# Polysketch attention and PReLU MLP on one core: the last MLP group written by token, and a fixed order of operations

## The chip, the core and the metric

The kernel runs on one core of a Trainium2 chip. A core has five engines, each with its own queue of instructions: TensorE (PE in the profile) multiplies matrices and writes to PSUM, eight banks of 128 x 512 fp32; VectorE (DVE), ScalarE (ACT) and GpSimd (POOL) work element by element; SyncE (SP) starts DMA transfers here, as ScalarE does for a few. An instruction waits in its queue until what it depends on is done, and everything behind it on that engine waits with it. The metric is the time of the program on the device in microseconds, median over runs.

## What is computed

Linear attention with a polynomial sketch for 4 batches of 4 heads, 1088 tokens, head dimension 32; then an MLP over all 4352 tokens (128 -> 2048 -> 128) with a PReLU whose slope alpha differs by hidden unit.

```python
def phi(x):
    a = np.einsum('rd,bhsd->bhsr', S1, x)
    b = np.einsum('rd,bhsd->bhsr', S2, x)
    return np.einsum('bhsi,bhsj->bhsij', a, b).reshape(*x.shape[:-1], r * r)
q_p, k_p = phi(q), phi(k)
num = np.einsum('bhsf,bhfd->bhsd', q_p, np.einsum('bhsf,bhsd->bhfd', k_p, v))
den = np.einsum('bhsf,bhf->bhs', q_p, np.sum(k_p, axis=2))[..., None] + 1e-06
x = (num / den).transpose(0, 2, 1, 3).reshape(B * S, H * D)
h = x @ w_in
out = (np.maximum(h, 0) + alpha * np.minimum(h, 0)) @ w_out
```

## The kernel before

**Algebra.** PReLU is alpha h + (1 - alpha) relu(h). So the kernel prepares W = w_in diag(alpha) w_out, a 128 x 128 matrix, and w_out scaled by 1 - alpha, and computes relu(x w_in) w_out' + x W.

**Attention, by batch.** `keys` transposes k in 32 x 32 blocks on VectorE, applies the sketches ("ab", on TensorE with small tiles of its array), forms phi on GpSimd, a Gram matrix for the sum of phi(k) ("gram"), and phi(k)^T v ("kv", L519), which is transposed ("tz") and copied to `kvw`. `queries` does the same for q ("qabc"), divides by the denominator, forms phi(q) and multiplies by kvw ("num", L610). The result is copied as bf16 into `xT`, 128 features by 4352 tokens (L619). Batch 0's queries are two units, the others one each.

**MLP, by group of tokens.** `GROUPS` are eight groups of 512 columns of xT and a last one of 256. For each of the 16 blocks of hidden units: a matmul of w_in's block with xT into one of the banks H0 to H2 (L633; A0 to A3 too in the last two groups), a relu into a bf16 buffer rh on ScalarE (L640) or VectorE (L642), and a matmul with w_out's block that accumulates in bank O (L646). A 17th matmul adds x W (L653). Bank O then holds the output with features on partitions; VectorE transposes it in 32 x 32 blocks into a buffer oT (L658), and four DMAs, one for each 32 features, write it in rows of 128 bytes (L670); a group that spans two batches needs eight. All are on SyncE's queue, but for two of the last group's, which are on ScalarE's.

**Preparation.** w_in is cast to bf16 in four pieces on ScalarE (L412). It is also transposed by TensorE in four pieces (L430), scaled by alpha into winT on VectorE or ScalarE (L438, L441), and multiplied by w_out (L448) into W, whose cast is on ScalarE (L451). w_out is scaled in L420 and L423.

**Order.** Every operation is an `Op` with engines, a duration, dependencies and the buffers that it takes. `schedule` picks one after the other: of those that could start first by its own clock, the one with the smallest number in `ORDER`; it also picks the engine and the buffer, and fills TensorE's gaps early in the program with matmuls on zeros (L382). The instructions are then issued in that order, so each engine's queue holds it. Loads of later batches are held back by tiny VectorE writes ("gates", L356) into their destination.

Of the kernel before, what the change touches and what calls it, by code (L numbers as in the profile page):

```python
# [12 lines left out]
BF16 = mybir.dt.bfloat16  # L13
# [15 lines left out]
SLACK = {"ACT": 140, "PE": 0, "DVE": 170}  # L29
# [3 lines left out]
ORDER = [  # L33
# [48 lines left out]
STICK = {"PE": 5000}  # L82


def schedule(ops, slots, filler=None):
# [4 lines left out]

    free_at = {"DVE": 830, "PE": 900, "POOL": 700, "ACT": 700}
    cfg, glued = "full", None
# [4 lines left out]
    def slot_free(s):  # L97
        h = holder[s]
        if h is None:
            return slot_at[s]  # L100
        if any(o.end is None for o in h.frees) or not h.frees:
            return None
        return max(o.end + 150 for o in h.frees)

    waits = {id(o): sum(d.end is None for d in o.deps) for o in ops}
    users = {}
    for o in ops:
        for d in o.deps:
            users.setdefault(id(d), []).append(o)
    ready = [o for o in ops if waits[id(o)] == 0]  # L110
    order = []
    while ready:
        best = None
        known = {}
        for o in ready:
            t0 = 0
            picks = []
            ok = True
            taken = set()
            for h in o.takes:  # L120
                for s in h.names:
                    if s not in known:
                        known[s] = slot_free(s)
                cand = sorted((known[s], s) for s in h.names if known[s] is not None and s not in taken)
                if len(cand) < h.n:
                    ok = False
                    break
                chosen = cand[:h.n]
                taken |= {s for _, s in chosen}
                picks.append([s for _, s in chosen])  # L130
                t0 = max([t0] + [t for t, _ in chosen])
            if not ok:
                continue
            for e, dur in o.eng.items():
                if e == "PE":
                    if glued is not None and o is not glued:
                        continue
                    if o.cfg != cfg:
                        dur += SWITCH
                    if free_at.get("PE", 0) < COLD and not o.warm:  # L140
                        dur *= 2
                t = max(t0, free_at.get(e, 0))
                if o.port and e in ("DVE", "POOL"):
                    t = max(t, free_at.get("PORT", 0))
                for d in o.deps:
                    t = max(t, d.end + (0 if d.on == e else d.lat if d.on == "DQ" else d.lat + SLACK.get(e, 0)))
                if e == "PE":
                    for i, (limit, at) in enumerate(have):
                        if issued + o.ni > limit:
                            t = max(t, have[i + 1][1])  # L150
                o_key = (t, o.prio, t + dur)
                if best is None:
                    best = []
                best.append((t, o.prio, t + dur, o, e, dur, picks))
        assert best, "no operation can start"

        t_first = min(b[0] for b in best)
        near = [b for b in best if b[0] <= t_first + 60]
        t, _, end, o, e, dur, picks = min(near, key=lambda b: (
            b[1] - (STICK["PE"] if b[4] == "PE" and b[3].cfg == cfg != "full" else 0), b[2]))  # L160
        if e == "PE" and filler and 4000 < free_at.get(e, 0) < FILL:
            each = 430 if free_at[e] < COLD else 215
            n = int((t - free_at[e] - 40) / each)
            idle = [s for s in FILL_BANKS if slot_free(s) is not None and slot_free(s) <= free_at[e]
                    and s not in sum(picks, [])]
            if n > 0 and idle:
                x = filler(n, idle[-1], each)
                x.behind = [f for f in holder[idle[-1]].frees] if holder[idle[-1]] else []
                x.end, x.on, x.took = free_at[e] + each * n, e, each * n
                order.append((free_at[e], e, x))  # L170
                slot_at[idle[-1]] = x.end
                holder[idle[-1]] = x.takes[0]
                issued += x.ni
                cfg = x.cfg
# [3 lines left out]
        if e == "PE":  # L178
            issued += o.ni
            cfg, glued = o.cfg, o.glue  # L180
            if issued > have[-1][0] - 256:
                have.append((have[-1][0] + 256, max(end, free_at.get("DQ", 0)) + 2600))
        for h, names in zip(o.takes, picks):
            h.got = names
            o.behind += [f for s in names if holder[s] for f in holder[s].frees]
            for s in names:
                holder[s] = h
        order.append((t, e, o))
        ready.remove(o)
        for u in users.get(id(o), ()):  # L190
            waits[id(u)] -= 1
            if waits[id(u)] == 0:
                ready.append(u)
# [5 lines left out]
def kernel(  # L199
# [12 lines left out]
    nc = tc.nc  # L212
# [511 lines left out]
```

## Time and profile before

| | |
|---|---|
| median of 3 runs | 106.33 us (105.56 to 108.42) |
| profiled execution | 106.62 us, span 103.9 us |
| busy: PE, weight loads, DVE, ACT, POOL | 96.5, 52.0, 71.3, 71.3, 43.3 us |
| granted TensorE clock | 0.998 |
| DMA | 11.24 MB, 22863 packets, 19008 of them under 512 bytes |
| the chain that ended last | PE 71%, DMA 8%, DVE 8%, SyncE's queue 6% of the span |

The span runs from the first instruction to the last; the profiled execution's time holds some 2.7 us more around it. Matmuls are pipelined: the record of one of 512 columns lasts 0.38 us, and the next starts 0.22 us after it, so PE's busy time covers short waits. Idle time of an engine that is not the bottleneck costs nothing.

### The profile page before, as it was taken

What the parts mean: (1) busy time and instruction counts of PE and PEld (TensorE: products, weight loads), DVE (VectorE), ACT (ScalarE), POOL (GpSimd) and SP (SyncE); (2) the same over time, 40 slices, a digit from 0 to 9 for tenths busy, and PEclk for the clock granted to TensorE, in tenths of its full rate; (3) what the DMA queues carried; (4) which work ended last, traced back from release to release, by engine and by line L of the source; (5) the groups of instructions that cost most, each with busy time, mean ns of one, the idle gap of its engine ahead of it and who ended that gap; (6) DMA issues with size and microseconds to landing.
All of it is one profiled execution on the core that took longest, in us unless ns stands there. A gap on an engine that the chain in (4) does not pass through costs nothing.

```text
span 103.9 us, 3351 instructions
## 1 busy us (share of the span) xinstructions
PE 96.5 (93%) x1364; PEld 52.0 (50%) x1375; DVE 71.3 (69%) x154; ACT 71.3 (69%) x157; POOL 43.3 (42%) x47
## 2 busy tenths in 40 slices
PE   5978999999999999999999997999999999999950
PEld 4637789544653444446453444444444344444740
DVE  3556999997999994867867963892365544654740
ACT  1331998396676996664967952899798898694820
POOL 4009619499937999099159629700000000000000
PEclk9999999999999999999999999999999999999999
DMA  2999974965200777075002380140033060032243
GB/s 64 311 218 362 415 288 137 290 199 172 102 0 6 109 227 197 11 125 192 0 0 40 60 212 17 26 75 0 6 47 54 0 95 9 7 61 36 39 65 51
DMA packets 22863, 11.24 MB, mean 108 GB/s; under 512 B 19008, under 2 KB 21056, under 8 KB 22848
## 3 DMA queue, kind: packets, MB, share of 16 engines
q1 hardware_dynamic: 21952, 10.95, 40.5%
q8 instruction: 10, 0.16, 0.6%
q10 hardware_dynamic: 896, 0.08, 0.6%
q14 instruction: 5, 0.04, 0.1%
HBM read 8.80 MB, written 2.23 MB: 106 GB/s over the span
## 4 chain that ended last, share of the span: by engine, by line
PE 71%; DMA 8%; DVE 8%; SPq 6%; issue 3%; ACT 1%; ACTq 0%
PE O L646 24%; PE H L633 23%; SPq L305 6%; PE A L610 5%; DMA q_sb<-in_q_dram 5%; PE A L633 3%; DMA v_sb<-in_v_dram 3%; PE H L519 3%; PE O L448 3%; PE A L555 2%; DVE winT L438 2%; PE O L653 2%; PE A L469 1%; PE A L519 1%; PE A L499 1%
## 5 line engine op out<-in xcount | busy, mean ns | idle before, releaser
L640 ACT ACTIVATE rh<-H 128x512 bf16<-128x512 f32 (+1 forms) x96 | 50.8, 595 | 8.1 <-PE H L633 6.5
L633 PE MATMUL H<-xT,w_in_bf 128*128 128x512 bf16 (+1 forms) x122 | 40.0, 374 | 0.4 <-DVE ab L476 0.2
L646 PE MATMUL O<-rh,w_out_bf 128*128 128x512 bf16 (+1 forms) x135 | 39.8, 366 | 0.4 <-issue 0.2
L642 DVE TENSOR_SCALAR rh<-H 128x512 bf16<-128x512 f32 (+1 forms) x28 | 18.3, 658 | 7.1 <-PE H L633 5.9
L633 PEld LDWEIGHTS <-w_in_bf 128*128 128x128 bf16 x144 | 13.7, 99 | 16.4 <-issue 3.2
L484 POOL TENSOR_TENSOR phi<-ab 128x576 f32<-128x576 f32 x15 | 17.3, 1179 | 10.7 <-DVE ab L476 10.7
L646 PEld LDWEIGHTS <-w_out_bf 128*128 128x128 bf16 x144 | 13.9, 98 | 15.2 <-issue 1.7
L590 POOL TENSOR_TENSOR qf<-qa 128x1152 f32<-128x1152 f32 (+2 forms) x9 | 17.0, 1908 | 3.6 <-DVE qa L583 3.3
L658 DVE STREAM_TRANSPOSE oT<-O 128x512 f32<-128x512 f32 (+1 forms) x9 | 6.1, 683 | 9.6 <-PE O L646 7.1
L596 DVE STREAM_TRANSPOSE qp<-qf 128x1152 f32<-128x1152 f32 (+2 forms) x10 | 11.1, 1119 | 0.0
L561 DVE STREAM_TRANSPOSE qa<-A 128x288 f32<-128x288 f32 (+2 forms) x20 | 7.0, 395 | 2.2 <-PE A L555 2.2
L640 ACT ACTIVATE rh<-A 128x512 bf16<-128x512 f32 (+1 forms) x13 | 5.8, 514 | 2.6 <-PE A L633 2.5
L382 PE MATMUL O<-warm 128*128 128x256 bf16 x36 | 6.3, 338 | 1.1 <-DVE warm L364 1.1
L610 PE MATMUL A<-qp,kvw 32*32 32x288 f32 (+2 forms) x320 | 7.1, 364 | 0.0
L461 DVE STREAM_TRANSPOSE kT<-k_sb 128x544 f32<-128x544 f32 x8 | 5.6, 720 | 1.6 <-DMA k_sb<-in_k_dram 1.5
L619 ACT CAST xT<-A 128x128 bf16<-128x128 f32 (+3 forms) x12 | 3.3, 332 | 4.9 <-PE A L610 4.9
L412 ACT CAST w_in_bf<-w_in_f 128x512 bf16<-128x512 f32 x4 | 4.4, 1147 | 3.2 <-DMA w_in_f<-in_moe_w_in_dram 3.2
L546 DVE STREAM_TRANSPOSE qT<-q_sb 128x544 f32<-128x544 f32 (+2 forms) x10 | 5.7, 602 | 1.0 <-DMA q_sb<-in_q_dram 1.0
L583 POOL TENSOR_TENSOR qa<-qa,rd 128x288 f32<-128x288 f32 (+1 forms) x4 | 2.5, 630 | 8.6 <-DVE rd L582 6.3
L619 DVE CAST xT<-A 128x288 bf16<-128x288 f32 (+2 forms) x8 | 2.9, 392 | 3.7 <-PE A L610 3.7
L610 PEld LDWEIGHTS A<-qp,kvw 32*32 32x32 f32 x320 | 3.9, 103 | 2.8 <-issue 1.3
L382 PEld LDWEIGHTS <-warm 128*128 128x128 bf16 x36 | 4.1, 121 | 2.2 <-DVE warm L364 1.1
(80 smaller groups left out, 86.7 us busy)
## 6 DMA issues: line engine op xcount, KB each, us to landing
k_sb<-in_k_dram SPq DMA_DIRECT2D x3, 544.0 KB, 4.7
q_sb<-in_q_dram SPq DMA_DIRECT2D x3, 544.0 KB, 4.1
out_dram<-oT SPq DMA_DIRECT2D x20, 64.0 KB, 2.0
v_sb<-in_v_dram SPq DMA_DIRECT2D x8, 144.0 KB, 3.7
v_sb<-in_v_dram SPq DMA_DIRECT2D x8, 128.0 KB, 4.0
w_in_f<-in_moe_w_in_dram SPq DMA_DIRECT2D x2, 512.0 KB, 6.7
w_out_f<-in_moe_w_out_dram SPq DMA_DIRECT2D x2, 512.0 KB, 5.5
k_sb<-in_k_dram SPq DMA_DIRECT2D x2, 272.0 KB, 3.0
```

The source lines that it names most:

```text
L305: getattr(nc, eng).dma_start(dst, src)
L382: nc.tensor.matmul(bank[name][:, :256], warm[:, :128], warm[:, :256], start=True, stop=True)
L484: eng.tensor_mul(bufs[hph.got[0]][:, rr_, :, h2].rearrange("p w (i j) -> p w i j", i=r), view(src, [[64, KW], [1, r], [0, r]], 32 * rr_ + ...
L561: ta.append(op(("DVE", dve(n)), lambda h=h: nc.vector.transpose(bufs[hqa.got[0]][:, h * n:(h + 1) * n], bank[hA[h].got[0]][:, :n]), prio + ...
L590: side(e).tensor_mul(bufs[hqf[rr_].got[0]][:, :4 * n].rearrange("p (m i j) -> p m i j", i=r, j=r), view(src, [[32, 2 * nb], [1, r], [0, r] ...
L596: mu.append(op(("DVE", dve(4 * n) + 40), lambda rr_=rr_: nc.vector.transpose(bufs[hqp[rr_].got[0]][:, :4 * n], bufs[hqf[rr_].got[0]][:, :4 ...
L610: nc.tensor.matmul(bank[hX[c].got[0]][32 * h:32 * (h + 1), :n], kvw[b][32 * c:32 * (c + 1), i, 32 * h:32 * (h + 1)], view(bufs[hqp[h // 2] ...
L619: x_done[x0] = (w, op({"ACT": act(w), "DVE": dve(w)}, lambda e, c=c, w=w, x0=x0: copy(e)(xT[:, x0:x0 + w], bank[hX[c].got[0]][:, :w]), lat ...
L633: hm = op(("PE", n / 2.4 + 3), lambda c=c, hh=hh: nc.tensor.matmul(bank[hh.got[0]][:, :n], w_in_bf[:, c * 128:(c + 1) * 128], xT[:, col0:c ...
L640: nc.scalar.activation(bufs[hr.got[0]][:, :n], bank[hh.got[0]][:, :n], ACTF.Relu)
L642: nc.vector.tensor_scalar_max(bufs[hr.got[0]][:, :n], bank[hh.got[0]][:, :n], 0.0)
L646: nc.tensor.matmul(bank["O"][:, :n], w_out_bf[:, c], bufs[hr.got[0]][:, :n], start=state["n"] == 0, stop=state["n"] == last)
```

## The change

**The last group's output is computed by token.** For the last 256 columns, the relu's result is the stationary operand and w_out's block the moving one: two matmuls of 128 columns for each of 16 blocks, and two for x W, each half into a bank of its own with 128 tokens on partitions. No transpose follows: each half is copied to a buffer and written by one DMA in rows of 512 bytes, the first from SyncE and the second from ScalarE. So that the tokens of a half lie well in the output, the last 256 columns of xT are permuted when they are copied from PSUM, which splits that copy in two. In the first eight blocks both halves are one operation, in the last eight two. The last group may use bank O for its hidden units, and there are twelve rh buffers instead of ten.

**The order is written out.** `ORDER` goes, and `PLAN` lists all 719 operations by number, with the engine where there is a choice (a, d, p). `schedule` walks through the list and assigns buffers by its own clock.

**Dependencies.** ScalarE's copies that may come first (`c_wq`, `c_g`, `c_win`) depend on `c_tab`, the copy that stands behind the table load, and the first entries of the plan are the loads of the sketch rows and of alpha.

```diff
-ORDER = [
-    -2000, -1990, 2, 3, 4, 5, 6, 7, 8, 9, 20000, 7003, 1007, 4992, -17950, 7045, 20000, 8112, -7780, -9037,
...
+PLAN = """
+    14 13 12 10 19 18 2 56 0 1 11 20 21 22 3 57 58 59 60 27 4 143 144 65 66 5 15 6 61p 63p 28 29 23 67 68d 32 41
...
+    order = []
+    for word in plan.split():
+        o = ops[int(word.rstrip("adp"))]
+        e = names[word[-1]] if word[-1] in names else next(iter(o.eng))
...
-    P_rh = pool("rh", 10, [128, 512], BF16)
+    P_rh = pool("rh", 12, [128, 512], BF16)
...
+            tail = GROUPS[-1][1] if x0 + w == T else 0
+            def f_x(e, c=c, w=w, x0=x0, tail=tail):
+                x = bank[hX[c].got[0]]
+                copy(e)(xT[:, x0:x0 + w - tail], x[:, :w - tail])
+                if tail:
+                    copy(e)(view(xT, [[128, tail // 128], [1, 4], [4, 32]], T - tail),
+                            x[:, w - tail:w].rearrange("p (t j i) -> p t j i", j=4, i=32))
...
+        hT = [Hold(ABANKS + ["O"]), Hold(ABANKS + ["O"])]
+        def by_token(i, x, w):
+            nc.tensor.matmul(bank[hT[i].got[0]][:, :DM], x, w, start=done[i] == 0, stop=done[i] == last)
+            done[i] += 1
...
+            def f_t(c=c, hr=hr, parts=(0, 1)):
+                for i in parts:
+                    by_token(i, bufs[hr.got[0]][:, 128 * i:128 * (i + 1)], w_out_bf[:, c])
...
+            for i, ts in enumerate((t0, t1)):
+                ho = Hold(P_ob)
+                ev = op({"DVE": dve(DM), "ACT": act(DM)}, lambda e, i=i, ho=ho: copy(e)(
+                    bufs[ho.got[0]][:, :4].rearrange("p a b -> p (a b)"), bank[hT[i].got[0]][:, :DM]),
+                    prio - 5, deps=os_ + ts, takes=[ho], frees=[hT[i]])
+                def f_rows(i=i, ho=ho):
+                    b, x = B - 1, col0 + 128 * i - (B - 1) * S
+                    dma(("sync", "scalar")[i], dram(out, (b * S + x // 32) * DM, [[NB * DM, 32], [1, 4 * DM]]),
+                        bufs[ho.got[0]][:, :4].rearrange("p a b -> p (a b)"))
```

**Where the order differs: ScalarE before the first relus.** Line numbers are those of each kernel. winT is w_in transposed and scaled, kvs and kvw are batch 0's copies, rh are relu buffers, A, H and O PSUM banks. Before:

```order
L412 CAST w_in_bf<-w_in_f 128x512 x3
L423 ACTIVATE w_out_bf<-w_out_f,oma 128x128 x4
L412 CAST w_in_bf<-w_in_f 128x512
L441 ACTIVATE winT<-H_104,al 128x128 x4
L423 ACTIVATE w_out_bf<-w_out_f,oma 128x128 x4
L451 CAST W_bf<-O 128x128
L619 CAST xT<-A_101 128x128
L619 CAST xT<-A_103 128x128
L619 CAST xT<-A_102 128x128
L640 ACTIVATE rh_130<-H_104 128x512
```

Now, from the second winT chunk on (a cast of w_in and one chunk stand ahead of it):

```order
L417 ACTIVATE winT<-O,al 128x128 x4
L417 ACTIVATE winT<-H_105,al 128x128 x4
L499 COPY kvs_116<-H_104 128x256
L388 CAST w_in_bf<-w_in_f 128x512
L508 COPY kvw_96<-H_106 128x256
L373 COPY Wq_90<-ST 128x16
L399 ACTIVATE w_out_bf<-w_out_f,oma 128x128 x4
L388 CAST w_in_bf<-w_in_f 128x512
L599 CAST xT<-A_102 128x128
L599 CAST xT<-A_100 128x128
L388 CAST w_in_bf<-w_in_f 128x512
L630 ACTIVATE rh_130<-H_106 128x512
```

Three winT chunks and the copies of batch 0 have come to ScalarE, one set of w_out's scalings and W's cast have moved behind the first relus, and three of the four w_in casts now stand behind the scalings.

**SyncE around batch 3's v (v_sb_73).** The oT writes here are those of the group that spans two batches, and after the change those of group 1. Before:

```order
L305 DMA q_sb<-in_q_dram 128x1088
L305 DMA out_dram<-oT_142 32x2x32 x4
L305 DMA out_dram<-oT_142 32x14x32 x4
L305 DMA v_sb_73<-in_v_dram 32x4x288
L305 DMA v_sb_73<-in_v_dram 32x4x256
L305 DMA v_sb_73<-in_v_dram 32x4x288
L305 DMA v_sb_73<-in_v_dram 32x4x256
```

Now:

```order
L281 DMA k_sb_69<-in_k_dram 128x1088
L281 DMA out_dram<-oT_143 32x16x32 x4
L281 DMA q_sb<-in_q_dram 128x1088
L281 DMA v_sb_73<-in_v_dram 32x4x288
L281 DMA v_sb_73<-in_v_dram 32x4x256
L281 DMA v_sb_73<-in_v_dram 32x4x288
L281 DMA v_sb_73<-in_v_dram 32x4x256
L281 DMA out_dram<-oT_144 32x2x32 x4
L281 DMA out_dram<-oT_144 32x14x32 x4
```

The loads of q and v of batch 3 stand behind one group's four writes, which precede them, and ahead of the writes of the group that spans two batches.

**SyncE and TensorE at the end.** oT_140 to oT_144 are output buffers. SyncE before:

```order
L305 DMA out_dram<-oT_142 32x16x32 x4
L305 DMA out_dram<-oT_140 32x6x32 x4
L305 DMA out_dram<-oT_140 32x10x32 x4
L305 DMA out_dram<-oT_141 32x16x32 x4
L305 DMA out_dram<-oT_142 32x8x32 x2
```

And now:

```order
L281 DMA out_dram<-oT_143 32x16x32 x4
L281 DMA out_dram<-oT_142 32x6x32 x4
L281 DMA out_dram<-oT_142 32x10x32 x4
L281 DMA out_dram<-oT_143 32x4x128
L281 DMA out_dram<-oT_144 32x16x32 x4
```

The first token half's write (4 x 128 in each of 32 rows) stands ahead of the four of group 7. TensorE's last rows before:

```order
L646 LDWEIGHTS w_out_bf
L646 MATMUL O<-rh_132,w_out_bf 128x256
L646 LDWEIGHTS w_out_bf
L646 MATMUL O<-rh_133,w_out_bf 128x256
L653 LDWEIGHTS W_bf
L653 MATMUL O<-xT,W_bf 128x256
```

And now, from group 7's last output matmul (L636) on; ten matmuls of the token halves (L617, into A_101 and A_102) follow it, of which the first five stand here:

```order
L636 LDWEIGHTS w_out_bf
L636 MATMUL O<-rh_130,w_out_bf 128x512
L617 LDWEIGHTS rh_135
L617 MATMUL A_102<-w_out_bf,rh_135 128x128
L617 LDWEIGHTS rh_136
L617 MATMUL A_101<-w_out_bf,rh_136 128x128
L617 LDWEIGHTS rh_133
L617 MATMUL A_101<-w_out_bf,rh_133 128x128
L617 LDWEIGHTS rh_139
L617 MATMUL A_101<-w_out_bf,rh_139 128x128
L617 LDWEIGHTS rh_141
L617 MATMUL A_101<-w_out_bf,rh_141 128x128
```

Group 7's accumulation ends close to the program's end. On VectorE its transpose is the last instruction, and ScalarE's last three are the two halves' copies and the second half's write.

More of the change, by code (lines that the diff above doesn't have):

```diff
@@ L102, in slot_free @@
             return None
[L103 to L107, printed above, removed]
-        for d in o.deps:
[L109 to L174, printed above, removed]
@@ new lines, in slot_free @@
+        return max(o.end + 100 for o in h.frees)
+    order = []
+    for word in plan.split():
+        o = ops[int(word.rstrip("adp"))]
+        e = names[word[-1]] if word[-1] in names else next(iter(o.eng))
+        dur = o.eng[e]
+        t, picks, taken = 0, [], set()
+        for h in o.takes:
+            cand = sorted((t_, s) for t_, s in ((slot_free(s), s) for s in h.names if s not in taken) if t_ is not None)
+            assert len(cand) >= h.n, "no buffer is free"
+            taken |= {s for _, s in cand[:h.n]}
+            picks.append([s for _, s in cand[:h.n]])
+            t = max([t] + [t_ for t_, _ in cand[:h.n]])
+        if e == "PE":
+            if o.cfg != cfg:
+                dur += SWITCH
+            if free_at["PE"] < COLD and not o.warm:
+                dur *= 2
+        t = max(t, free_at[e])
+        if o.port and e in ("DVE", "POOL"):
+            t = max(t, free_at["PORT"])
+        for d in o.deps:
+            t = max(t, d.end + (0 if d.on == e else d.lat))
+        if e == "PE":
+            for i, (limit, at) in enumerate(have):
+                if issued + o.ni > limit:
+                    t = max(t, have[i + 1][1])
+            if 4000 < free_at[e] < FILL:
+                each = 430 if free_at[e] < COLD else 215
+                n = int((t - free_at[e] - 40) / each)
+                idle = [s for s in FILL_BANKS if slot_free(s) is not None and slot_free(s) <= free_at[e]
+                        and s not in sum(picks, [])]
+                if n > 0 and idle:
+                    x = filler(n, idle[-1], each)
+                    x.behind = list(holder[idle[-1]].frees) if holder[idle[-1]] else []
+                    x.end, x.on, x.took = free_at[e] + each * n, e, each * n
+                    order.append((free_at[e], e, x))
+                    holder[idle[-1]], slot_at[idle[-1]] = x.takes[0], x.end
+                    issued += x.ni
+        end = t + dur
```

102 lines of the change are left out of this document (68 added, 34 removed), and 14 rows, old and new, of the table ORDER.

## The prediction

> **What bounds the kernel now.** I read the busy time by stages first, to see which engine a stage belongs to. The columns are the stretch's length and then the busy time (and instructions) of PE, of its weight loads, of DVE, ACT and POOL; the 1.00 is the granted clock.
>
> ```profile
> 10.00:20.40 10.40, 10.23 (x266) 8.36 (x266) 10.01 (x29) 8.54 (x20) 5.63 (x7) 1.00 0.81 288
> 20.40:60.00 39.60, 38.87 (x645) 18.93 (x645) 33.40 (x75) 29.63 (x65) 29.38 (x25) 1.00 0.39 97
> 60.00:66.00 6.00, 5.33 (x148) 2.99 (x148) 2.81 (x7) 2.72 (x8) 4.13 (x3) 1.00 0.35 96
> 66.00:96.00 30.00, 29.75 (x193) 13.31 (x194) 16.55 (x25) 25.10 (x50) 0.86 (x1) 1.00 0.23 36
> 96.00:100.20 4.20, 4.15 (x35) 3.11 (x32) 2.79 (x8) 3.00 (x10) 0.00 (x0) 1.00 0.41 64
> ```
>
> From 10 us, when the first half of w_in has landed, until the last matmul at 100 us, TensorE is the bound: it is idle 0.17 + 0.73 + 0.67 + 0.25 + 0.05 = 1.87 us of 90.2. The granted clock is 1.00 throughout. No reordering can therefore win more than about two microseconds there; the remaining places are the 3.9 us after the last matmul and the 10 us before w_in.
>
> The chain of waits (start, length, what) shows the largest of the idle pieces, at 62.7 us: batch 3's kv matmuls (L519) wait for its v, whose four loads stand in SyncE's queue behind eight output writes, which stand behind a transpose of VectorE.
>
> ```profile
> 53.12 0.73 DVE oT L658
> ...
> 59.96 3.27 DMA v_sb<-in_v_dram
> 63.37 1.40 PE H L519 x72
> ```
>
> The end, from the timeline: last matmul, transpose of the output, two writes on each of two queues. The row below it gives KB and microseconds from issue to landing.
>
> ```profile
> 99.87 0.27 PE L653 MATMUL O<-xT,W_bf 128*128 128x256 bf16 x1
> 100.18 0.45 DVE L658 STREAM_TRANSPOSE oT<-O 128x256 f32<-128x256 f32 x1 [0.66 <-PE O L653]
> 100.66 0.81 SPq L305 DMA_DIRECT2D out_dram<-oT  x2
> 100.67 0.88 ACTq L305 DMA_DIRECT2D out_dram<-oT  x2
> ...
> out_dram<-oT ACTq DMA_DIRECT2D x2, 32.0 KB, 1.8
> ```
>
> Count everything from P, the start of the last matmul (99.87). The last issue starts at about 100.67 + 0.88/2 = 101.1, that is P + 1.2, and lands 1.8 us on, at P + 3.0; the span's other 1.0 us is the program's end, the same in both kernels.
>
> **The change, part by part.** The profiled execution took 106.62 us for a span of 103.9; the median of the runs is 106.33. I sum in the profile's time and take 0.3 off for the median at the end.
>
> *The head, up to the first MLP matmul.* The new order moves the scaling of w_in's transposes (winT) from three on VectorE and one on ScalarE to one and three, and puts the last four W matmuls behind the attention's first outputs.
>
> ```profile
> 10.03 3.26 ACT L412 CAST w_in_bf<-w_in_f 128x512 bf16<-128x512 f32 x3 [3.23 <-DMA w_in_f<-in_moe_w_in_dram]
> 13.19 1.27 ACT L423 ACTIVATE w_out_bf<-w_out_f,oma 128x128 bf16<-128x128 f32 x4
> 15.42 1.12 ACT L441 ACTIVATE winT<-H,al 128x128 f32<-128x128 f32 x4
> 19.25 0.60 ACT L619 CAST xT<-A 128x128 bf16<-128x128 f32 x3 [0.68 <-PE A L610]
> ...
> L523 ACT COPY kvs<-H 128x256 f32<-128x256 f32 x2 | 0.7, 372 | 3.3 <-PE H L519 3.3
> ...
> 20.48 0.16 issue
> 20.64 0.38 PE H L633
> ```
>
> TensorE still starts on w_in at 10.05, since that load stands where it stood, and has the same work to do; what can go is the 0.17 us of idle time and the 0.16 before 20.64: 0.3 us. Against it, ScalarE now has four casts (3.26/3 each), three winT chunks (1.12 each), one set of w_out scalings (1.27), three copies (up to 0.37 each) and two xT copies (0.2 each) ahead of its first relu: 10.0 + 4.3 + 3.4 + 1.3 + 1.1 + 0.4 = 20.5, while the first MLP matmul, which now comes ahead of the next queries' matmuls, can start from about 19.9. W_bf's cast now stands behind three relus, and the first output matmul needs it, since W and the output share bank O. I charge 0.3 us for that [0 to 0.6]. The head comes out even.
>
> *The MLP stretch.* The idle 0.73 + 0.67 + 0.25 = 1.65 us from 20.4 to 96 is what a better order can take. Most of 60 to 66 is the wait for v. In the new order SyncE issues q and v of batch 3 ahead of group 2's eight writes, but behind group 1's four; and TensorE wants v earlier.
>
> ```profile
> 43.17 1.96 SPq L305 DMA_DIRECT2D out_dram<-oT  x4
> 45.23 0.45 SPq L305 DMA_DIRECT2D q_sb<-in_q_dram  x1
> 59.00 1.87 SPq L305 DMA_DIRECT2D v_sb<-in_v_dram  x4
> ...
> DMA to landing us min/median/max: 3.2/4.0/5.3
> ...
> 42.50 0.57 PE A L499 x36
> 43.07 0.65 PE A L469 x16
> ...
> 45.25 0.70 PE A L555 x32
> ...
> 46.52 1.28 PE H L519 x72
> ...
> 92.77 3.24 PE O L646 x15
> ```
>
> A 512-column matmul costs 3.24/15 = 0.216 us. Group 1's last output matmul comes, in both orders, after 35 w_in and 34 output matmuls. The old order reaches that point at 42.50; the new one has put three pieces ahead of it that followed it before, gram, kv and ab of the next batches: 42.5 + 0.57 + 1.28 + 0.65 = 45.0. The transpose is 0.73 more and ends near 45.9, the four writes hold SyncE until 47.9, q until 48.4, and the last of the four v loads starts about 49.8 and lands 3.2 to 4.0 later, at 53.0 to 53.8. TensorE reaches the kv matmuls after 28 more of 0.216, a gram (0.57), a set of query matmuls (0.70) and two small pieces (0.4, my estimate): 45.0 + 6.0 + 1.7 = 52.7. The wait is not gone; it moves and shrinks, to 0.4 us [0 to 1.1].
>
> The relus move from ScalarE to VectorE: 35 to 46 there, 109 to 98 here, ten of the eleven 512 wide.
>
> ```profile
> L642 DVE TENSOR_SCALAR rh<-H 128x512 bf16<-128x512 f32 x26 | 17.6, 678 | 7.1 <-PE H L633 5.9 <-PE O L646 1.1
> ```
>
> Ten at 0.678 are 6.8 us more for VectorE. Between 66 and 96 it is idle 30 - 16.55 = 13.4 us and three quarters of the additional ones stand there; they hide. Before 60 it has 6.2 us free of 39.6 and gets three more, 2.0 us: they hide on average, but a late transpose can hold up TensorE. Twelve relu buffers in place of ten give some slack. I charge 0.4 us for new waits of this kind [0 to 1.5]. Together the stretch gains 1.65 - 0.4 - 0.4 = 0.85.
>
> *The last group spread among group 7.* Now its 33 matmuls come in one piece and wait for relus:
>
> ```profile
> 96.06 0.38 PE L633 MATMUL A<-xT,w_in_bf 128*128 128x256 bf16 x2
> ...
> 98.34 1.69 PE L646 MATMUL O<-rh,w_out_bf 128*128 128x256 bf16 x14
> ```
>
> Fourteen take 1.69 with the last one's 0.27, so one is (1.69 - 0.27)/13 = 0.109. From 96.06 to P there are 32 of them, 3.49 us, and it took 3.81: 0.32 lost. Among group 7's matmuls the relus have cover, so this goes; the one place without cover is the relu of the last w_in matmul on ScalarE, 0.1. Gain 0.2.
>
> *The output by token.* 17 matmuls of 256 columns become 34 of 128, each with its own weights, and the relu's result is now the weights. The extra ScalarE copy that permutes the last 256 columns of xT lies far ahead of its use. What does a pair of load and 128-column matmul cost? The streaming is half of 0.109, 0.054; the load is either hidden under it or not.
>
> ```profile
> L646 PEld LDWEIGHTS <-w_out_bf 128*128 128x128 bf16 x144 | 13.9, 98 | 15.2 <-issue 1.7
> ...
> L610 PEld LDWEIGHTS A<-qp,kvw 32*32 32x32 f32 x320 | 3.9, 103 | 2.8 <-issue 1.3 <-DVE rd L578 0.4
> ...
> L430 PEld LDWEIGHTS H<-ident,w_in_f 128*128 128x128 f32 x16 | 2.0, 194 | 0.4 <-DMA w_in_f<-in_moe_w_in_dram 0.2 <-issue 0.2
> ```
>
> No such pair is in the trace. The bounds are 0.054 (hidden, as at 256 columns) and 0.109 (a load needs as long as the shortest pair seen). Of fp32, 96 more columns cost 194 - 103 = 91 ns, so some 73 ns of a load are fixed latency that overlaps, and a bf16 load of 98 ns has about 25 ns of real loading, well under 54. I take 0.056: 34 x 0.056 - 17 x 0.109 = +0.05 us [0 to +1.85].
>
> [...]
>
> *The end.* The token halves need no transpose, a ScalarE copy each, and one write each, the second on ScalarE's queue. But the new order ends differently. Group 7's last output matmul stands ten 128-column matmuls before the end, VectorE's transpose of it is that engine's last instruction, and its four writes of 64 KB are SyncE's last, behind the first token half's write.
>
> ```profile
> 6.54 0.27 ACT L404 COPY G<-H 128x128 f32<-128x128 f32 x1 [0.68 <-PE H L402]
> L658 DVE STREAM_TRANSPOSE oT<-O 128x512 f32<-128x512 f32 x8 | 5.7, 712 | 9.0 <-PE O L646 7.1 <-PE O L653 1.9
> out_dram<-oT SPq DMA_DIRECT2D x20, 64.0 KB, 2.0
> ```
>
> From P: the first half's last matmul starts four before it, P - 0.2, is seen 0.26 later, is copied in 0.27, so its write is issued at P + 0.35 and holds SyncE until about P + 0.8. Group 7's matmul starts at P - 0.7, its transpose runs from P - 0.3 to P + 0.4, so its writes wait for SyncE, not for data. Four of them take 1.96 us; the last starts near P + 2.2 and lands 2.0 later, P + 4.2, against P + 3.0 now. Cost +1.2 us [+0.9 to +1.3]; it would be 0.4 less if the token half's write stood last. That the second half's write is issued by ScalarE at P + 0.6 gains nothing then.
>
> *Alpha's load ahead of the table load* changes nothing: the table load already follows it.
>
> ```profile
> 1.68 0.42 ACTq L305 DMA_DIRECT2D al<-in_moe_alpha_dram  x1
> 2.13 1.28 ACT L366 ACT_TABLE_LOAD   x1 [2.13 <-issue]
> ```
>
> Sum: head 0, stretch -0.85, last group -0.2, load pairs +0.05, end +1.2: +0.2. 106.62 + 0.2 - 0.3 = 106.5 us for the median.
>
> **The rivals.** *The order runs dense.* No new waits at all: -0.3 - 1.65 - 0.3 + 0.05, and the end at its lower bound, +0.9, make -1.3: 105.0. For it: TensorE is busy 29.75 of 30 us in 66 to 96 under the old order already, and the plan interleaves more evenly. Against it: v behind group 1's writes, worked out above. Below 104.2 it comes only if the end costs nothing, too.
>
> *Loads that don't hide.* If a pair takes 0.109, the 34 add 1.85 rather than 0.05: 108.3, and with one late relu in the last stretch 108.5 or more. It decides from about 0.11 us a pair. For it: no pair of 128 columns is in the trace and the pace at 256 is 0.109. Against it: the 25 ns from the fp32 rows. [...]
>
> *VectorE late between 20 and 60 us.* With 6.2 us of slack and 2.0 more work, transposes that TensorE needs could queue behind relus in each of three batches, 0.7 us each (VectorE's 0.678 a relu): +2.1 less the 0.4 already charged, 108.2.
>
> **How the numbers follow.** About 2% (2.1 us) is what a measurement of this kernel can tell from no change, whose three runs lie 2.9 us apart. My forecast, 105.6 to 107.5, has 0.55; the dense order 0.22, of which I put 0.12 below 104.2; the loads 0.11 and the late VectorE 0.12, of which together 0.15 above 108.45. So faster 0.12, within 2% 0.73, slower 0.15. The range for 8 in 10 takes in the dense order at 105.0 and the loads at 108.3, without the tails beyond.
>
> **What would show it.** Right: PE idle under 1.2 us after 20 us; 128-column matmuls 56 ns apart; SyncE's last four issues starting 0.8 us after the last matmul and the last landing near P + 4.2; a short wait for v near 52 us. Wrong: pairs at 80 to 110 ns; a first MLP matmul later than 21 us; waits of TensorE for VectorE between 20 and 60; or a last landing at P + 3 or sooner, which would put the whole near 105.

## The result, and the profile after

The changed kernel is slower: a median of 110.23 us (109.38 to 110.90, four runs) beside 106.56 us for the kernel before (105.56 to 108.42, four runs). The ratio is 1.037, 95% interval 1.026 to 1.049; it, and every ratio below, leaves out runs over 1.5% longer than the fastest of the same kernel. The prediction of 106.5 us, and its range up to 108.3, were too low.

The profiled execution of after took 110.43 us, with a span of 108.3 us (before: 106.62 and 103.9). Its busy time by stages, in the columns that the prediction explains (length, then PE, weight loads, DVE, ACT, POOL, then the granted clock, DMA share and GB/s):

```profile
10.00:20.40 10.40, 10.04 (x236) 7.96 (x234) 9.34 (x27) 9.28 (x26) 5.68 (x7) 1.00 0.64 223
20.40:52.00 31.60, 31.23 (x571) 15.38 (x575) 26.03 (x59) 24.56 (x57) 22.65 (x23) 1.00 0.44 118
52.00:55.14 3.14, 0.84 (x38) 0.52 (x37) 2.96 (x8) 0.04 (x1) 2.75 (x3) 1.00 0.75 190
55.14:58.91 3.77, 3.31 (x75) 2.46 (x77) 0.44 (x1) 0.81 (x3) 2.72 (x2) 0.55 0.02 4
58.91:66.00 7.09, 7.04 (x94) 3.12 (x97) 5.90 (x10) 5.73 (x13) 0.79 (x1) 1.00 0.24 37
66.00:96.00 30.00, 29.74 (x226) 13.77 (x225) 22.66 (x36) 22.31 (x45) 4.98 (x3) 1.00 0.24 37
96.00:102.86 6.86, 6.80 (x62) 4.52 (x60) 4.44 (x10) 4.37 (x11) 0.00 (x0) 1.00 0.24 40
```

Four of the seven stretches are 98 to 99% busy on TensorE, as the dense ones of before, and in the first it idles 0.36 us where it idled 0.17. Two stand out. From 52.00 to 55.14 us TensorE is busy 0.84 of 3.14 us, and from 55.14 to 58.91 it is busy, but at a granted clock of 0.55. The waits name the first (engine, line, what it waited for: us in all, times, longest), and the chain shows both:

```profile
PE A L495 <- DMA v_sb<-in_v_dram: 2.3, 1, 2.3
```

```profile
50.15 4.86 DMA v_sb<-in_v_dram
55.01 0.14 issue
55.14 0.32 PE A L495 x8
55.46 0.12 issue
55.58 1.93 PE A L495 x64
57.51 0.33 issue
57.85 1.06 PE H L623 x2
58.91 0.72 PE O L636 x3
59.63 0.12 PE A L485 x2
```

Batch 3's kv matmuls (L495) wait 2.3 us for v, and 64 of them another 0.12, until the last of v's four loads has landed at 55.45; the kernel before waited 0.6 us for the same data. Then the 64 take 1.93 us and the next two MLP matmuls 1.06. A later run of the same kernel ("the changed kernel again", below) shows the same matmuls with the clock at 1.00:

```profile
54.80 1.10 PE A L495 x64
55.90 0.32 PE O L636
56.22 0.43 PE H L623 x2
56.66 0.65 PE O L636 x3
57.30 0.12 PE A L485 x2
```

There the 64 take 1.10 us and the two 0.43. (The 0.33 us of "issue" at 57.51 stands where this run has an output matmul of 0.32 us; in the first trace its record is missing.) So TensorE ran at half clock here, which the kernel before did not do until 103.49 us, after its last matmul.

Why v comes so late stands on SyncE's queue (start, busy us, DMA issues; then durations of one issue in ns, min/median/max):

```profile
45.59 3.00 SPq L281 DMA_DIRECT2D out_dram<-oT  x4
48.70 0.45 SPq L281 DMA_DIRECT2D q_sb<-in_q_dram  x1
49.25 1.81 SPq L281 DMA_DIRECT2D v_sb<-in_v_dram  x4
```

```profile
L281 SPq DMA_DIRECT2D out_dram<-oT x4: 332/484/1554, 45.6 to 48.1; - x4
```

The queue order is the one that the prediction worked through, and the writes start near where it put them, at 45.6 us. But they hold SyncE 3.00 us, not 1.96, because the third took 1554 ns to issue instead of some 490. Then v takes longer to land: 4.7 to 4.9 us from its issue, with q's 544 KB issued directly ahead of it.

The end, from the timeline:

```profile
102.13 0.72 PE L617 MATMUL A<-w_out_bf,rh 128*128 128x128 bf16 x10
102.33 0.72 DVE L679 STREAM_TRANSPOSE oT<-O 128x512 f32<-128x512 f32 x1 [1.27 <-PE O L636]
102.67 0.49 ACT L662 COPY oT<-A 128x128 f32<-128x128 f32 x2 [0.55 <-PE A L617]
102.96 2.93 SPq L281 DMA_DIRECT2D out_dram<-oT  x5
103.18 0.64 ACTq L281 DMA_DIRECT2D out_dram<-oT  x1
```

Ten matmuls of 128 columns, 0.056 us apart, put the start of the last one (P) at 102.13 + 9 x 0.056 = 102.63. SyncE then issues five writes for 2.93 us, and the span ends at P + 5.65; before, it ended at P + 4.0.

So the span grew by 4.4 us, and it divides like this: P came 2.76 us later (102.63 against 99.87), the end is 1.65 us longer. Of the 2.76, the wait for v is 2.3 + 0.1 - 0.6 = +1.8. The half clock is +1.55: from the first of the 64 kv matmuls to L485 TensorE took 59.63 - 55.58 = 4.05 us, in the later run 57.30 - 54.80 = 2.50. That leaves -0.6 for everything else. The whole execution grew by 3.8 only, because 0.6 us less lies outside the span; why is not known.

### The profile page after: what moved, and what is told of

It reads as the page before. It is cut to its first block, busy times and chain, and to the rows that moved or that the text cites. A ratio compares the mean times of both kernels' runs of the same rounds, so it can differ in the third digit from the quotient of the medians.

```text
span 108.3 us, 3386 instructions
## 1 busy us (share of the span) xinstructions
PE 97.5 (90%) x1381; PEld 53.3 (49%) x1392; DVE 77.4 (71%) x163; ACT 69.8 (64%) x156; POOL 43.4 (40%) x47
## 4 chain that ended last, share of the span: by engine, by line
PE 79%; DVE 8%; DMA 4%; issue 3%; SPq 1%; ACT 0%; DVEq 0%
PE H L623 23%; PE O L636 23%; PE A L586 6%; DMA v_sb<-in_v_dram 4%; PE O L358 4%; PE A L623 4%; PE A L495 3%; PE O L424 3%; PE A L531 2%; PE A L445 2%; PE A L617 2%; PE O L674 2%; DVE qa L537 1%; PE H L495 1%; DVE phi L460 1%
## 5 line engine op out<-in xcount | busy, mean ns | idle before, releaser
L630 ACT ACTIVATE rh<-H 128x512 bf16<-128x512 f32 (+1 forms) x87 | 46.8, 589 | 11.3 <-PE H L623 10.2
L623 PE MATMUL H<-xT,w_in_bf 128*128 128x512 bf16 (+1 forms) x121 | 38.4, 376 | 0.6 <-issue 0.5
L636 PE MATMUL O<-rh,w_out_bf 128*128 128x512 bf16 x120 | 37.7, 380 | 0.3 <-issue 0.2
L632 DVE TENSOR_SCALAR rh<-H 128x512 bf16<-128x512 f32 (+1 forms) x36 | 23.6, 660 | 6.7 <-PE H L623 5.8
L636 PEld LDWEIGHTS <-w_out_bf 128*128 128x128 bf16 x128 | 12.5, 99 | 14.8 <-issue 3.4
L679 DVE STREAM_TRANSPOSE oT<-O 128x512 f32<-128x512 f32 x8 | 5.7, 715 | 3.7 <-PE O L636 3.7
L632 DVE TENSOR_SCALAR rh<-A 128x512 bf16<-128x512 f32 (+1 forms) x10 | 5.7, 576 | 1.7 <-PE A L623 1.6
L623 PE MATMUL A<-xT,w_in_bf 128*128 128x512 bf16 (+1 forms) x21 | 6.8, 338 | 0.1
L552 POOL TENSOR_TENSOR qa<-qa 128x288 f32<-128x288 f32 (+1 forms) x4 | 2.9, 728 | 9.1 <-DVE qa L537 9.1
L495 PE MATMUL A<-phi,v_sb 128*32 128x64 f32 (+1 forms) x144 | 3.6, 262 | 2.4 <-DMA v_sb<-in_v_dram 2.3
L599 ACT CAST xT<-A 128x128 bf16<-128x128 f32 (+4 forms) x12 | 3.3, 327 | 3.5 <-PE A L586 3.4
```

The source lines that it names most:

```text
L495: nc.tensor.matmul(bank[hK.got[0]][32 * h:32 * (h + 1), :R], v_sb[b][rows_, h, w], bufs[hph.got[0]][rows_, h // 2, w, h % 2], start=(w == ...
L623: hm = op(("PE", n / 2.4 + 3), lambda c=c, hh=hh: nc.tensor.matmul(bank[hh.got[0]][:, :n], w_in_bf[:, c * 128:(c + 1) * 128], xT[:, col0:c ...
L630: nc.scalar.activation(bufs[hr.got[0]][:, :n], bank[hh.got[0]][:, :n], ACTF.Relu)
L632: nc.vector.tensor_scalar_max(bufs[hr.got[0]][:, :n], bank[hh.got[0]][:, :n], 0.0)
L636: nc.tensor.matmul(bank["O"][:, :n], w_out_bf[:, c], bufs[hr.got[0]][:, :n], start=state["n"] == 0, stop=state["n"] == last)
L679: ev = op(("DVE", dve(n)), lambda: nc.vector.transpose(bufs[ho.got[0]][:, :nb].rearrange("p a b -> p (a b)"), bank["O"][:, :n]), prio - 5, ...
```

## The experiments

**v early.** Undoes one step: batch 3's v loads behind its k load, instead of behind group 1's writes and q.

```diff
-        load_batch(b, ab_, z_, kv_) if b > 1 else load_batch(b, z_, kv_, kv_)
+        load_batch(b, ab_, z_, kv_ if b < 3 else ab_) if b > 1 else load_batch(b, z_, kv_, kv_)
 PLAN: the words 124 and 125 (v's gate and loads) moved from behind 119d and 136 to behind 121 (batch 3's k load)
```

> The changed kernel with one move: batch 3's v loads, and the gate on VectorE that releases them, stand right behind batch 3's k load (issued near 35 us) instead of behind group 1's writes and the q load (49.2 us). Theory A (the late v costs twice: TensorE waits 2.4 us for it, and the granted clock then falls to half for some 3 us, which costs 2.0 more): both go, 110.2 - 4.4 = 105.8 us, the clock stays 1.00 between 53 and 59 us. Theory B (the clock falls there for a reason of its own, such as the load on the chip): only the wait goes, 107.8 us, with the clock still at half somewhere near 55. Theory C (the loss lies in the order's other waits, VectorE late): hardly any change, 109.5 us or more.

Measured: 106.5 us, ratio to before 1.007 (1.003 to 1.011). The v loads went out at 40.1 us, since the gate's new place on VectorE comes a little later than meant, and landed 2.5 to 4.0 us after their issue with nothing in front. TensorE no longer waited for v, its clock stayed at 1.00 from 50 to 60 us, and the last matmul came at 98.98 us, 3.65 us earlier than in the changed kernel. Theory A stands, B and C fall: the wait and the clock go together. Of the 4.4 us that theory A foresaw, 3.7 came: the half clock is worth some 1.6 us and not 2.0, and TensorE was already 0.5 us later than in the changed kernel when it came to batch 3's keys (L475 at 52.67 against 52.20).

**Zeros in the wait.** Keeps v late, but TensorE busy.

```diff
         def kvm(w0, w1):
+            if b == B - 1: zeros(11, hK.got[0])
```

> The changed kernel with 22 matmuls of 256 columns of zeros (0.109 us each, 2.4 us) put ahead of batch 3's kv matmuls, into the bank that these overwrite; the v loads stay late. Theory A (the clock falls because TensorE stood idle 2.4 us): v still lands near 55.0 us and kv starts then, but at a clock of 1.00, so 2.0 us come back: 108.2 us. Theory B (the clock falls for another reason): it still falls, 110.2 us or a little more.

Measured: 109.0 us (108.85 to 109.23). TensorE's rows there:

```profile
52.97 2.58 PE L358 MATMUL A<-warm 128*128 128x256 bf16 x22
55.47 1.35 PE L495 MATMUL A<-phi,v_sb 64*32 64x64 f32 x72
```

The 72 kv matmuls take 1.35 us, the clock is 1.00 until after the last matmul. So it was the idle TensorE that lost the clock, as theory A has it. It missed the 108.2 by 0.8 us, for two reasons. The half clock had been charged at 2.0 us and is worth some 1.6. And the zeros ended at 55.47, while v's last load had landed by 54.9 (issued at 50.3, landing 4.5 us later), so they ran past it by some 0.5 us.

**Half the zeros.** The same with zeros(6, ...).

> The changed kernel with 12 matmuls of zeros (1.3 us) ahead of batch 3's kv, so that TensorE idles about 1.0 us for v instead of 2.3. If what drops the clock is the idle share of a fixed stretch of time (the records have the clock change on a grid of 3.41 us; two thirds of one such stretch were idle in the changed kernel's profile), a third is not enough: no drop, 108.6 us. If any idle of a microsecond drops it, half clock for 3.4 us again: 110.2.

Measured: 109.0 us, but its four runs go from 107.63 to 110.66. In the profiled one (108.46) the zeros end at 54.3, kv starts at 55.01, and the clock holds. The run of 110.66 shows a mean clock of 0.975, so something dropped it there; without a trace of that run it cannot be said where. Inconclusive.

**q and v ahead of the writes.** One word moved.

```diff
 PLAN: the word 350 (group 1's writes) moved from behind 349 to behind 125 (batch 3's v loads)
```

> The changed kernel with one swap on SyncE's queue: q and v of batch 3 ahead of group 1's four writes; their gates on VectorE stay at 45.6 and 46.5 us. In the changed kernel one of the four writes took 1.55 us to issue instead of 0.49, while a fetch of 16 KB of instructions ran at 46.7 us. Theory A (an issue that meets an instruction fetch is stretched by the fetch): now q's or a v load's issue is stretched by about 1 us, the last v issue starts near 49.0, v lands near 53.2 (4.2 later), TensorE waits 0.4 us, the clock holds, 106.2 us. Theory B (the long issue belongs to the third of four writes, or to the DMA queue being full): no long issue among q and v, the last v issue starts near 48.0, lands near 52.2, no wait, 105.8 us, and the long issue is still among the writes.

Measured: 106.9 us, ratio 1.010 (1.005 to 1.014), no wait for v. SyncE's issues, and the durations of one in ns:

```profile
45.94 0.35 SPq L281 DMA_DIRECT2D q_sb<-in_q_dram  x1
46.91 2.69 SPq L281 DMA_DIRECT2D v_sb<-in_v_dram  x4
```

```profile
L281 SPq DMA_DIRECT2D v_sb<-in_v_dram x4: 328/426/1357, 46.9 to 49.2; - x4
```

The long issue has left the writes (1554 ns in the changed kernel) and sits on a v load (1357 ns), at 47.3 us; between 47 and 49 us the trace has one packet of an instruction queue, of 0.02 MB and some 1.0 us (3.1% of 16 engines' 2 us). Theory A stands on that: in these two runs the stretch belonged to the moment, not to the kind of transfer. Its 0.4 us of waiting did not come; with the kv matmuls at 53.1 us, v was there. The profiled run took 106.44 us; the median is 0.7 us above theory A's 106.2, and why is not known.

**By token alone.** The kernel before with the last group's output form of the change and nothing else; the order of before is kept.

```diff
+        def by_token(x, w):
+            for i in range(2):
+                nc.tensor.matmul(bank["O"][:, 128 * i:128 * i + DM], x[:, 128 * i:128 * i + 128], w,
+                                 start=state["n"] == 0, stop=state["n"] == last, skip_group_check=True)
...
-        ev = op(("DVE", dve(n)), lambda: nc.vector.transpose(
+        ev = op(("DVE", dve(n)), lambda: (nc.vector.tensor_copy if tokens else nc.vector.transpose)(
...
+                    dma(("sync", "scalar")[i], dram(out, (b * S + x // 32) * DM, [[NB * DM, 32], [1, 4 * DM]]),
+                        bufs[ho.got[0]][:, 4 * i:4 * i + 4].rearrange("p a b -> p (a b)"))
```

> The kernel before with the last group's output by token alone: 34 matmuls of 128 columns for 17 of 256, one copy of 256 columns for the transpose, one write of 64 KB in rows of 512 bytes on each of the two queues for two; the order is the old one to the last instruction. Theory A (loads hide, the form costs and earns next to nothing; the loss is the order's): matmuls 0.056 us apart, +0.05 us on TensorE, an end as long as before within 0.3 us: 105.9 us, ratio 1.000 within 0.004. Theory B (part of the loss is the form's): pairs of 0.08 to 0.11 us or an end 1 us longer, ratio 1.008 to 1.018.

Measured: ratio 1.001 (0.998 to 1.005). Its end:

```profile
98.64 0.94 PE L642 MATMUL O<-w_out_bf,rh 128*128 128x128 bf16 x14
...
100.18 0.65 SPq L305 DMA_DIRECT2D out_dram<-oT  x1
100.19 0.66 ACTq L305 DMA_DIRECT2D out_dram<-oT  x1
```

Fourteen matmuls in 0.94 us with the last one's 0.22 give (0.94 - 0.22)/13 = 0.055 us each. On each queue one write of 64 KB takes 0.65 us to issue, where two of 32 KB took 0.81 (SyncE) and 0.88 (ScalarE). Within the interval the form costs and earns nothing: the loss is the order's.

**alpha late.** The v-early kernel with alpha's load behind ScalarE's table load.

```diff
 PLAN: the word 1 (alpha's load) moved from behind 0 to behind 11 (the table load's copy)
```

> The first experiment's kernel (v early) with the third part of the change undone: alpha's load stands behind ScalarE's table load and its first copy, so it is issued near 3.6 us instead of 1.7 and lands near 8.9 instead of 7.1. Theory A (alpha has slack: its first reader starts at 10.7 us): no change against v early, ratio to the kernel before 1.007. Theory B (SyncE's w_out loads, which in the changed kernel sat 1.9 us waiting for alpha's landing, go out 1.8 us later, and the output matmuls' weights with them): the first output matmul, at 22.7 us in the changed kernel, comes up to 1 us later, ratio up to 1.016.

Measured: ratio 1.006 (1.001 to 1.011), beside v early's 1.007. But the edit did not move the load. ScalarE's queue in alpha late, and alpha's load in v early:

```profile
1.69 1.28 ACT L342 ACT_TABLE_LOAD   x1 [1.69 <-PEq L727]
1.75 0.41 ACTq L281 DMA_DIRECT2D al<-in_moe_alpha_dram  x1
```

```profile
1.68 0.42 ACTq L281 DMA_DIRECT2D al<-in_moe_alpha_dram  x1
```

Alpha's load now stands behind the table load and is issued at 1.75 us all the same, while the table load runs, and lands 5.2 us later (5.4 in v early); it was meant to go out near 3.6. So neither theory was tested: whether alpha has slack stays open.

**The changed kernel again.**

> The changed kernel unaltered, for more runs of it beside the others on one chip. If the late v costs 2.4 us of waiting in every run and the fall of the clock 2.0 us more in those runs whose grid of 3.41 us lies so that some two thirds of one stretch are idle, the spans fall into two heaps about 1 to 2 us apart, the longer with a mean clock of 0.98 or less, the shorter with 0.99; median 109.5 to 110.2 us, ratio 1.035.

Measured: median 109.33 us over six runs; the ratio of 1.027 (1.019 to 1.035) is that of the three shortest. With the first four there are ten: four at a mean clock of 0.99 or more take 108.0 to 109.4 us, six at 0.982 or less take 109.9 to 111.6: two heaps, as expected. The profile is of the fastest, 108.04 us:

```profile
45.79 1.96 SPq L281 DMA_DIRECT2D out_dram<-oT  x4
47.84 0.89 SPq L281 DMA_DIRECT2D q_sb<-in_q_dram  x1
48.83 1.80 SPq L281 DMA_DIRECT2D v_sb<-in_v_dram  x4
```

```profile
PE A L495 <- DMA v_sb<-in_v_dram: 1.5, 2, 1.3
```

Here it was q's issue, at 47.84 us, that was long, 0.89 us instead of 0.45, and none of the writes (1.96 us, as the prediction had it). TensorE waited 1.5 us instead of 2.3 and kept its clock; the 64 kv matmuls took 1.10 us.

**The end's writes dealt out anew.** On the changed kernel.

```diff
-                    dma(("sync", "scalar")[i], dram(out, (b * S + x // 32) * DM, [[NB * DM, 32], [1, 4 * DM]]),
+                    dma("scalar", dram(out, (b * S + x // 32) * DM, [[NB * DM, 32], [1, 4 * DM]]),
...
-                    dma("sync", dram(out, (b * S + j0) * DM + 32 * dq, [[NB * DM, 32], [DM, j1 - j0], [1, 32]]),
+                    dma("scalar" if g == 7 and dq == 3 else "sync", dram(out, (b * S + j0) * DM + 32 * dq, [[NB * DM, 32], [DM, j1 - j0], [1, 32]]),
 PLAN: the last words are 704 712 700 715a 717a 716 718 656
```

> The changed kernel with its last six writes dealt out anew: three of group 7's four on SyncE's queue with nothing ahead of them, both token halves and then group 7's fourth on ScalarE's. If the end is set by the six writes' issue (SyncE's last one starts at 105.38 us), the last issue moves to about 104.1 and the time falls by 1.2 us to 109.0. If it is set by something else (the landing of 64 KB in pieces of 128 bytes, or the program's end), it stays at 110.2.

Measured: 109.7 us median, four runs from 107.28 to 110.22, without a ratio. In the profile the last issue came at 103.56, P + 1.6, as meant, but the span still ended at P + 5.4: 0.3 us was gained of the 1.2. The third write on ScalarE's queue landed its last packet 3.8 us after P. The issue alone did not set the end.

**Early tail.** v early, and the last two groups in another order.

```diff
-    P_rh = pool("rh", 12, [128, 512], BF16)
+    P_rh = pool("rh", 16, [128, 512], BF16)
...
-                    dma(("sync", "scalar")[i], dram(out, (b * S + x // 32) * DM, [[NB * DM, 32], [1, 4 * DM]]),
+                    dma("scalar", dram(out, (b * S + x // 32) * DM, [[NB * DM, 32], [1, 4 * DM]]),
 PLAN from 714 on: 714 648 649a 705 620 706a 689 626 683 647 701 635 690d 710d 693 654 694d 672 668
 661a 680 650 655 702a 669 673a 670a 677 662 687 688 713 707 695 665 684 692 708 696 711 712 699 700
 691 674 703 704 671 715a 717d 716 718 656
```

> The first experiment's kernel (v early) with a new order of the last two groups: group 7's last w_in matmul and its last output matmuls stand about 1.5 us earlier on TensorE, ahead of most of the token matmuls; both token halves are written from ScalarE's queue, so that group 7's four writes have SyncE's to themselves; 16 relu buffers, one of the two token copies on VectorE, one relu moved from VectorE to ScalarE. Theory (the end is set by group 7's four writes, which start 1.1 us after the last matmul's start, P, and end the span at P + 5.6): they start before P, the token halves' writes become the last to land, near P + 3.6, and the span ends near P + 4.8: 0.8 us less than the 106.5 of v early, 105.7 us, ratio to the kernel before 0.998. If TensorE now waits for relus at the end, that is given back: 106.5.

Measured: 106.3 us, ratio 1.003 (0.999 to 1.006). TensorE waited for no relu, and group 7's writes started at 98.38, before P at 98.94. Yet the span ended at P + 5.3. SyncE shows why:

```profile
98.38 3.54 SPq L281 DMA_DIRECT2D out_dram<-oT  x4
```

```profile
SPq L281 <- DMA out_dram<-oT: 1.8, 1, 1.8
```

The fourth write stood until 101.61 us, for another write's completion: the trace gives it the same completion semaphore (109) as the first token half's write on ScalarE's queue.

**Early tail, written in another order.** PLAN ends in 656 715a 717d 716 718.

> The early tail's kernel, with group 7's four writes written into the program ahead of the token halves' two; no engine's own order changes by it, only which of the eight completion semaphores each write is given. In the early tail, SyncE's fourth write stood 1.8 us idle until 101.6 us, because its semaphore was that of the first token half's write. If that is why the end missed its 0.8 us, the fourth write now starts 0.9 us after P, the last landing comes near P + 3.6 instead of P + 4.1, and the span ends near P + 4.8: 105.8 us, ratio to the kernel before 0.997. If the write waited for something else, it stays at 106.3 and 1.0025.

Measured: 106.4 us, ratio 1.003 (0.999 to 1.007), the fourth write at 101.79. The edit did not do what it was for: both writes were still given the same semaphore. It repeats the early tail.

**Early tail, six semaphores.** PLAN ends in 715a 717d 718 716 656, so the second half is written first.

> The early tail's kernel with the two token halves' writes exchanged on ScalarE's queue (the second half first), by which the last six writes get six different completion semaphores; all else is the same. In the early tail and in its repeat, group 7's fourth write waited on SyncE until 101.6 us and 101.8 us, 2.7 and 2.6 us after P, and its semaphore was the one of the first token half's write. If that wait is what kept the end long, the fourth write now starts near P + 0.9, the last landing comes near P + 3.1 instead of P + 4.1, and the span ends near P + 4.4: 105.4 us, ratio to the kernel before 0.994. If the fourth write waits for something else, it stays at 106.3 and 1.0025.

Measured: 105.34 us, ratio to the kernel before 0.993 (0.990 to 0.996). That is 0.7% less than the kernel before, and less than the changed one.

```profile
98.36 1.95 SPq L281 DMA_DIRECT2D out_dram<-oT  x4
```

The four writes now go out in 1.95 us, the last packet lands at P + 3.0, and the span ends at P + 4.4, as expected. Of the last six writes only this fourth one moved by more than 0.2 us, from P + 2.67 to P + 0.88: the shared semaphore was the 0.9 us.

## Why the prediction was wrong

The span was to grow by 0.2 us and grew by 4.4. Of the 4.2 between, 2.0 are the wait for v, 1.55 the clock, 0.45 the end and 0.2 the rest.

**The wait for v** is the step that failed first: it was to shrink from 0.6 us to 0.4 and came to 2.4. The prediction put the four writes on SyncE until 47.9, the last v load at 49.8 and its landing 3.2 to 4.0 us later; TensorE would arrive at 52.7 and wait 0.4 us, 1.1 at most. TensorE arrived as foretold (its last matmul before the wait was issued at 52.65). The last v load started at 50.62, 0.8 late, because one write's issue took 1.1 us longer, and v landed up to 4.9 us after its issue, not 4.0. The 3.2 and 4.0 were the shortest and the median of a row whose longest, 5.3, was left out. Here q's 544 KB went directly ahead, and in "q and v ahead of the writes" v's landings behind q took 3.9 to 5.0 us, in v early with nothing in front 2.5 to 4.0; but in the kernel before batch 1's v followed its q within 0.7 us and landed in 3.7 to 3.8, so that q alone makes the difference is not shown. An issue of 1.733 us was in the trace of before, too, at 56.1 us, among the eight writes that stood ahead of v there, and the prediction passed over it.

**The clock** was missing altogether. The prediction read 1.00 in every stretch and treated a wait as worth its length. It was worth some 1.6 us more in the profiled run, where the clock was 0.50 for 3.41 us. The zeros, with which it stayed at 1.00, show that the idle time caused it, v early that it went with the wait.

**The end** was right in mechanism, with group 7's four writes behind a token half's on SyncE, but sized 1.2 us, 1.3 at most, against 1.65 measured. The first half's write held SyncE 0.65 us, not 0.45, and the four started at P + 1.07, not P + 0.8, and took 2.2 us, not 1.96.

**The rest held.** The head, the other waits, the spread last group and the load pairs were to bring together -1.65 + 0.6 + 0.4 - 0.2 + 0.05 = -0.8 us, and brought -0.6; their shares were not measured one by one. The pairs came 0.056 us apart, the value taken, so the bound of 0.109 was rightly not used. No wait of TensorE for VectorE longer than 0.3 us is left between 20 and 60 us, so the rival of a late VectorE is out, although its 108.2 us, like the loads' 108.3, came nearer than the forecast: the time alone would have pointed at the wrong rivals. No wait for W_bf shows either, for which 0.3 us were charged. The dense order was nearly there: with v early it runs without a wait from 20 us to the last matmul, 0.9 us sooner than before, and the end takes that back, which is why that kernel is 0.7% slower and not faster.

## What to carry to other kernels

A load that is needed at a fixed time is worth moving ahead of writes on the same queue, even when the sum says that it just arrives: here the queue's spread (an issue of 1.55 us instead of 0.48, a landing after 4.9 us instead of 4.0) was larger than the margin, and the idle TensorE lost its clock on top (0.50 for 3.41 us). When a few writes decide the end, look at which completion semaphore each write has been given (one shared by two of them cost 0.9 us here), as well as at which queue. A by-token output saves a transpose and writes longer rows, but here the two together were worth no time (ratio 1.001).

## What the runs showed of the hardware

**Long issues went with instruction fetches.** In the profiles of before and of the changed kernel, SyncE's and ScalarE's queues made 160 DMA issues. All five that took 0.9 us or more (0.91 and 1.73 us before; 1.24, 1.32 and 1.55 after) are SyncE's and overlap one of the 16 KB fetches that appear on an instruction queue, 0.88 to 1.36 us long in these two profiles; of the 145 that overlap none, the longest is 0.69 us and the median 0.43. The fetch of the changed kernel's long write, from 46.69 to 47.65 us, is seen among the queues of that stretch (46 to 49 us: packets, MB, share of 16 engines):

```profile
q8 instruction: 1, 0.02, 2.0%
```

Overlap alone does not suffice: the other ten issues that touch such a fetch take less than 0.9 us. That the long issue stays near 47 us when the writes there change places with q and v speaks for the fetch as its cause; no run moved a fetch.

**The clock fell behind stretches in which TensorE was little busy.** In the changed kernel's records the clock falls at 55.51 us and returns at 58.92, 3.41 us later. The full clock lasts 51.20 us before that and 47.79 us behind it, and 98.99 us in the profile of before: 15, 14 and 29 times as long. The 3.41 us before the fall in the changed kernel, with those behind it, and the 3.42 us before the fall at the end of the early tail (length, PE busy, ..., clock):

```profile
52.10:55.51 3.41, 1.06 (x45) 0.67 (x44) 3.23 (x8) 0.00 (x0) 3.02 (x3) 1.00 0.66 163
55.51:58.92 3.41, 3.00 (x67) 2.30 (x69) 0.07 (x1) 0.82 (x3) 2.35 (x2) 0.50 0.02 5
```

```profile
97.98:101.40 3.42, 1.18 (x22) 1.00 (x18) 0.67 (x2) 0.41 (x2) 0.00 (x0) 1.00 0.46 80
```

TensorE was busy 31% and 35% of the stretches before the falls. In the kernel with the end's writes dealt out anew it idled 2.4 us as well, but across two stretches of this length, 78% and 51% busy, and kept its clock:

```profile
51.02:54.43 3.41, 2.66 (x46) 1.25 (x44) 2.12 (x5) 1.70 (x4) 2.69 (x5) 1.00 0.98 264
54.43:57.85 3.42, 1.75 (x74) 1.36 (x75) 2.20 (x5) 0.28 (x2) 3.42 (x2) 1.00 0.20 44
57.85:61.26 3.41, 3.41 (x47) 1.50 (x46) 2.12 (x4) 2.87 (x8) 0.84 (x1) 1.00 0.02 2
```

So a wait of 2.3 us brought 1.55 us of half clock with it in the one profile, and a wait of 2.4 us none in the other. Two more stretches were about half busy. In alpha late's profile one that was 47% busy, with a wait for w_in in it, lost the clock; in the changed kernel again one of 46%, at its end, kept it (the next is still at 1.00):

```profile
7.96:11.37 3.41, 1.60 (x43) 1.09 (x39) 2.78 (x8) 0.37 (x2) 3.41 (x4) 1.00 0.92 336
11.37:14.78 3.41, 3.09 (x43) 2.38 (x44) 1.01 (x3) 2.23 (x5) 0.01 (x1) 0.50 1.05 376
```

```profile
98.96:102.38 3.42, 1.57 (x19) 1.04 (x17) 0.72 (x1) 1.21 (x5) 0.00 (x0) 1.00 0.10 29
102.38:105.79 3.41, 0.00 (x0) 0.00 (x0) 0.00 (x0) 0.00 (x0) 0.00 (x0) 1.00 0.54 86
```

In the profiles of before and of the changed kernel, every other full stretch of 3.41 us up to the start of the last matmul, counted from where the record of the clock begins (4.50 and 4.31 us), was at least 80% busy, and the clock was 1.00 behind each. The busy share does not tell the 46% from the 47%, and no run was made to find what does.
